# Fewer warm-up matmuls, x transposed by halves, and the first projections by column chunks, in a kernel of gated attention and feed-forward

## The chip, the cores and the metric

One core of a Trainium2 chip. The core has a matrix engine (TensorE, PE in the views; its weight loads are PEld), a vector engine (VectorE, DVE), a scalar engine (ScalarE, ACT), a general engine (GpSimd, POOL) and SyncE (SP), which issues most of the transfers. Each engine works through its own queue in order. The metric is device time of one launch in microseconds, lower is better.

## The reference

The input x has 2048 tokens of width 512. The output mixes two branches by a gate per token.

```python
x = A_x
g = _sigmoid((x * gate_w).sum(-1, keepdims=True))
a = _A_ref(x, A_wq, A_wk, A_wv, A_wo, A_beta)
b = _B_ref(x, B_W_gate, B_W_up, B_W_down)
return g * a + (1 - g) * b
```

Branch a is attention with 32 heads of width 16 in four segments of 512 tokens. In a segment each query attends causally to the keys of its own segment (softmax) and reads a memory of the earlier segments, a linear attention with phi(t) = t + 1 for t > 0 and exp(t) otherwise; a head's sigmoid(beta) mixes the two. At the end of a segment its keys and values are added to the memory. Branch b is a feed-forward net of width 1792: relu(x W_gate) times (x W_up), times W_down.

## The kernel before

**Tiles and stages.** The four segments (L = 512 tokens) are worked through with overlap. For a segment there are projections q, k and v (`proj_q`, `proj_k`, `proj_v`; four columns each, four matmuls of 128 x 512 to a column), attention by groups of eight heads (`attention`: score matmuls, an exponential on ScalarE, a causal mask on GpSimd, the product with v, then `normalise` on VectorE), `recall` and `memory` for the segments before, fourteen columns of the feed-forward net (`ffn_tasks`), and four output tiles (`out_tile`), which sum both branches in one PSUM bank. Matmuls of projections, feed-forward net and output all go through the helper `matmuls` (line 468), which cuts a sum into tasks of two matmuls (GM = 2); line 468 in a view is therefore any of them, and the operands tell which.

**The order.** Nothing is scheduled by the compiler. Every piece of work is a task in a list (`plan.add`) with an engine, an estimated duration, a key, the tasks it depends on and the PSUM banks or buffers it needs. `Plan.run` plays the list through with these estimates and picks, on each engine, the ready task with the lowest key; the instructions are then emitted in that order. Arrivals of transfers are tasks too, with estimated landing times in `LANDS`. A table `SHIFT` adds a number to the keys of single tasks, named by their place in the list. One unit of the key is 16,000 for the projections and the feed-forward net and 14,800 for attention.

**The start.** The transfers are issued first: x of segment 0 in two halves of tokens (`load_halves`, line 303, one half on SyncE's queue and one on ScalarE's), wq in two halves of its rows in the same way, then wk on SyncE's and wv on ScalarE's queue, then the feed-forward weights, gate_w, and x of the later segments, which a transposing transfer brings in as xT. For segment 0 xT is made on the chip instead (`x0_tasks`, line 479): TensorE first runs ten matmuls on a tile of zeros (`heat`, line 777; they write PSUM banks that nobody reads), then sixteen 128 x 128 transposes, four to each of the four column chunks of x, into one PSUM bank per chunk. Each chunk is copied to xT when its four transposes are done, chunks 0 and 2 by VectorE, 1 and 3 by ScalarE (line 492). In the plan the transposes wait for both halves of x, and every projection of segment 0 waits for all four copies and, for q, for both halves of wq. The gate's sums over x (line 420, four per segment, on VectorE) read the untransposed x.

Of the kernel before, what the change touches and what calls it, by code (L numbers as in the profile page):

```python
# [7 lines left out]
BF16 = mybir.dt.bfloat16  # L8
# [21 lines left out]
RH = 16  # L30

SHIFT = {
    21: -90000, 25: -170000, 29: -240000, 31: 210000, 52: 30000, 55: -10000, 58: -140000,
    74: 40000, 81: 90000, 85: 33000, 87: 80000, 88: -40000, 94: -80000, 115: 80000, 121: 100000,
    145: 130000, 204: -20000, 207: -50000, 210: -20000, 213: -3000, 222: -20000, 227: 270000,
    231: 1500, 234: 15600, 237: 30000, 240: -120000, 243: 11999, 246: 2000, 249: -10000,
    252: -14000, 255: 12999, 261: 28000, 264: -2000, 267: 30000, 270: 15000, 273: 28000,
    276: -10000, 279: 20000, 282: -2000, 300: -120000, 312: 24999, 324: -80000, 339: 80000,
    351: -50000, 354: 60000, 364: -20000, 372: -20000, 377: -50000, 379: 70000, 380: -40000,
    383: -100000, 385: 20000, 398: 10000, 400: 100000, 401: 10000, 404: 16000, 406: -130000,  # L40
    407: -4000, 480: -200000, 481: -190000, 544: 50000, 553: -18000, 556: 6000, 559: -30000,
    562: 2000, 565: -10000, 574: 19000, 583: -20000, 586: -10000, 589: -30000, 592: 9000,
    595: 10000, 598: 27000, 604: 2000, 607: -10000, 610: -4000, 613: -3000, 619: -10000,
    628: 21000, 631: -10000, 637: 29999, 661: 69999, 673: 70000, 686: 180000, 687: 150000,
    688: 100000, 689: -100000, 701: -120000, 704: 140000, 705: 110000, 709: -280000, 714: 15000,
    722: -6000, 727: -60000, 735: 15000, 737: 150000, 748: 8000, 751: -90000, 754: -60000,
    757: -10000, 796: -180000, 800: 90000, 801: 10000, 830: -160000, 831: -20000, 834: 140000,
    869: 30000, 903: 5000, 906: 40000, 909: -3000, 915: -15000, 921: -20000, 924: -10000,
    927: 10000, 930: 30000, 933: 10000, 936: 30000, 942: 30000, 945: -30000, 951: -10000,
    957: -20000, 963: -30000, 969: -20000, 972: 30000, 978: 40000, 984: 24000, 987: 209999,  # L50
    999: 110000, 1011: 60000, 1037: -230000, 1038: 60000, 1039: -260000, 1042: -100000,
    1046: -60000, 1047: 50000, 1052: -40000, 1054: -90000, 1057: 30000, 1062: -80000,
    1067: 56000, 1072: -60000, 1077: -50000, 1082: -70000, 1090: 50000, 1093: -20000,
    1096: 20000, 1134: -30000, 1170: 40000, 1239: 14000, 1242: 90000, 1247: 119999, 1248: 99999,
    1251: 10000, 1254: 60000, 1257: -20000, 1263: -2000, 1266: 20000, 1272: 50000, 1275: 60000,
    1278: 140000, 1284: 50000, 1290: 20000, 1293: -70000, 1296: -30000, 1299: -30000,
    1323: 159999,
}


# [154 lines left out]
def kernel(  # L215
# [69 lines left out]
    def work():  # L285
        return plan.one("ps", range(7, -1, -1))


    LANDS = dict(n0=4500, q=5950, k=9300, v=9750, g0=11800, u0=13300, gw=13900, g1=15200, u1=16700,
                 x1=18400, g2=20400, u2=21600, g3=22800, u3=24000, d0=27700, d1=30400, o=31800, n1=33400,  # L290
                 x2=35200)

    def arrival(name):
        return plan.add("in_" + name, 0.0, 0.0, None, lat=LANDS[name])

# [7 lines left out]
    def load_halves(dst, src, k, name):  # L303
        src = src.rearrange("(c p) n -> p c n", p=P)
        nc.sync.dma_start(out=dst[:, 0:k // 2], in_=src[:, 0:k // 2])
        nc.scalar.dma_start(out=dst[:, k // 2:k], in_=src[:, k // 2:k])
        return arrival(name)

    def load_xT(seg):
        nc.sync.dma_start_transpose(out=xT[seg % 3][:], in_=x[seg * L:(seg + 1) * L, :])  # L310
# [13 lines left out]
        return load(nc.sync, wd_sb[:, a:b, :],  # L324
                    B_W_down.rearrange("(c p) n -> p c n", p=P)[:, a:b, :], name)

    got_n[0] = load_halves(xn[0], x[0:L, :], 4, "n0")
    got_q = load_halves(wq_sb, A_wq, NC, "q")
    got_k = load_cols(nc.sync, wk_sb, A_wk, 0, D, "k")
    got_v = load_cols(nc.scalar, wv_sb, A_wv, 0, D, "v")  # L330
# [3 lines left out]
    got_gw = arrival("gw")  # L334
    load_gu(1)
    load_xT(1)
    got_x[1] = [arrival("x1")]
    junk = sb([P, L], BF16, "junk")
    nc.vector.memset(junk[:], 0.0)
    load_gu(2)  # L340
# [1 line left out]
    got_d = [load_wd(0, 7, "d0"), load_wd(7, NF, "d1")]  # L342
    got_o = load_cols(nc.sync, wo_sb, A_wo, 0, D, "o")
    load_xn(1)
    got_n[1] = arrival("n1")
    load_xT(2)
    got_x[2] = [arrival("x2")]
    plan.add("SP", 33100, -1e9, None)


# [64 lines left out]
    def gate_tasks(seg):  # L415
# [3 lines left out]
        for t in range(4):  # L419
            zs.append(plan.add("DVE", 690, key, lambda t=t: nc.vector.scalar_tensor_tensor(  # L420
                junk[:], xn[seg % 2][:, t, :], 1.0, gwb[:], ALU.mult, ALU.mult,
                accum_out=zc[:, 4 * seg + t:4 * seg + t + 1]), [got_n[seg], got_gw], 60, lock=True))
        att["xn", seg] = zs
        b = plan.add("DVE", 90, key, lambda: nc.vector.tensor_scalar(
            zc[:, cols], zc[:, cols], 80.0, -80.0, ALU.min, ALU.max), zs, DVL, lock=True)
# [33 lines left out]
            lock=seg > 0)  # L459


    def matmuls(key, deps, sl, ops, start=True, stop=True, prev=None, width=L, need=()):
        n = len(ops)
        for k in range(0, n, GM):
            def emit(k=k):
                for q in range(k, min(k + GM, n)):
                    lhsT, rhs = ops[q]()
                    nc.tensor.matmul(bank(sl)[:, 0:width], lhsT=lhsT, rhs=rhs,  # L468
                                     start=(start and q == 0), stop=(stop and q == n - 1))
            first = prev is None  # L470
            m = min(k + GM, n) - k
            t = plan.add("PE", 215.8 * width / L * m, key - (0 if first else CONT), emit, deps,
                         PEL, need=[sl] + list(need) if first else ())
            if not first:
                t.deps.append((prev, 0.0))
            prev, deps = t, ()
        return prev

    def x0_tasks():
        done = []  # L480
        for c in range(NC):
            sl = work()

            def pe(c=c, sl=sl):
                tp = bank(sl).bitcast(BF16)
                for t in range(4):
                    nc.tensor.transpose(tp[:, t * P:(t + 1) * P], xn[0][:, t, c * P:(c + 1) * P],
                                        ident[:])
            a = plan.add("PE", 240, K(-9), pe, [got_n[0]], PEL, need=[sl])
            cp = nc.scalar.copy if c % 2 else nc.vector.tensor_copy  # L490
            done.append(plan.add(
                "ACT" if c % 2 else "DVE", 430, K(-9), lambda c=c, sl=sl, cp=cp: cp(  # L492
                    xT[0][:, c, :], bank(sl).bitcast(BF16)[:, 0:L]),
                [a], DVL, frees=[sl]))
        return done

    def proj_mm(w, c, seg):
        return [lambda ci=ci: (w[:, ci, c * P:(c + 1) * P], xT[seg % 3][:, ci, :])
# [11 lines left out]
    def proj_q(seg, c):  # L510
        u, sl = 4 * seg + c, work()
        i = u % RQ
        key = K(4 * seg + c - 2 - (2 if seg else 0))
        war = [att.get(("pv", u - RQ)), att.get(("recall", u - RQ))]
        a = matmuls(key, got_x[seg] + [got_q] + war, sl, proj_mm(wq_sb, c, seg))
        xread.append(a)
        prj["q", seg, c] = plan.add("DVE", 600, key - RQK, lambda: nc.vector.tensor_copy(  # L517
            QT[i][:], bank(sl)), [a], DVL, frees=[sl])
        if seg:
            es, b = phi_exp(key, sl, a)  # L520
            prj["pq", seg, c] = plan.add("DVE", 665, key + 500, lambda: phi(
                pqT[i][:], QT[i][:], ex1[es.i][:]), [b, prj["q", seg, c]], DVL, frees=[es],
                lock=True)

    def proj_k(seg, c):
        i, u, sl = seg % 2, 4 * seg + c, work()
        key = K(4 * seg + c - 2 - (2 if seg else 0), 10)
        war = [att.get(("pv", u - RQ)), att.get(("recall", u - RQ))]
        a = matmuls(key, got_x[seg] + [got_k] + war, sl, proj_mm(wk_sb, c, seg))
        xread.append(a)  # L530
        ks = plan.one("ktr")
        d = plan.add("DVE", 600, key - RQK, lambda: nc.vector.tensor_copy(ktr[ks.i][:], bank(sl)),  # L532
# [242 lines left out]
    warm = [plan.one("ps") for _ in range(8)]  # L775

    def heat():
        for k in range(10):
            nc.tensor.matmul(bank(warm[k % 8]), lhsT=junk[:, 0:P], rhs=junk[:], start=True,  # L779
                             stop=True)  # L780
    plan.add("PE", 5280, -1e9, heat, lat=0, need=warm, frees=warm)
    got_x[0] = x0_tasks()
    for seg in range(NSEG):
        if seg > 1:
            got_n[seg] = plan.add("SP", 520, KA(4 * seg - 4), lambda seg=seg: load_xn(seg),
                                  att.get(("xn", seg - 2), []), 3500)
        if seg == 3:
            got_x[seg] = [plan.add("SP", 1900, K(4 * seg - 6), lambda seg=seg: load_xT(seg),
                                   list(xr0), 2200)]
        gate_tasks(seg)  # L790
        for c in range(NC):
            proj_q(seg, c)
            proj_k(seg, c)
        for t in range(4):
            proj_v(seg, t)
        for c in range(NC):
            if seg:
                recall(seg, c)
            attention(seg, c)
            if seg < NSEG - 1 and c == MEM:  # L800
                memory(seg, 4 * seg + c)
        ffn_tasks(seg)
        if seg == 0:
            xr0 = list(xread)
# [37 lines left out]
```

The softmax here doesn't subtract the row's maximum and nothing guards it: scores larger than these inputs give would overflow.

## Time and profile before

| | |
|---|---|
| median of 13 runs | 278.47 us (278.33 to 280.68) |
| the profiled execution's own time | 278.12 us |
| its span, first to last instruction | 276.3 us |
| busy: TensorE / VectorE / ScalarE / GpSimd | 265.4 / 207.7 / 195.9 / 87.3 us |
| first warm-up matmul starts | 1.25 us |
| first transpose of x starts | 5.49 us |
| first projection matmul starts | 7.46 us |
| first score matmul starts | 13.44 us |

Times in the profile count from the span's start. A row of the view in time gives start, duration, engine, line of the kernel, operation, what is written and read, and how many; in brackets stands how long the engine had been idle and what ended that. Matmuls overlap in their records, so their durations add up to more than the time they take; their pace is read from the distance of their starts. The chain of waits follows the work that ended last back to the start. The view by stretches gives busy time of each engine between two moments.

### The profile page before, as it was taken

The numbers are of one execution on the slowest core, as the hardware profiler recorded it, in microseconds if no ns is written. First come the engines' busy times: TensorE is split into PE (matmuls) and PEld (weight loads), VectorE is DVE, ScalarE is ACT, GpSimd is POOL, SyncE is SP. The second block draws the span as 40 slices with busy tenths as digits, with TensorE's granted clock in tenths as the row PEclk, the third lists the DMA queues.
The fourth block names the chain that finished last, engine by engine and source line by source line (L and its number), as shares of the span: only waits on it lengthen the run. The fifth ranks groups of instructions, "written<-read, shape, count | busy, mean of one in ns | idle before, by whom it ended". The sixth has DMA issues, their size and how long they took to land.

```text
span 276.3 us, 5510 instructions
## 1 busy us (share of the span) xinstructions
PE 265.4 (96%) x2178; PEld 113.3 (41%) x2214; DVE 207.7 (75%) x456; ACT 195.9 (71%) x176; POOL 87.3 (32%) x139
## 2 busy tenths in 40 slices
PE   8899999989999999999999999999999999999995
PEld 4343444433343433434343434343444334344543
DVE  3688989999898869698998768999228785638322
ACT  2299898968897778899996878778847776734100
POOL 5013333432424342534333343333301435230000
PEclk9999999999999999999999999999999999999999
DMA  7999955100411100100001000000000000000001
GB/s 234 328 281 346 258 81 168 11 15 0 96 23 20 23 19 21 21 0 19 4 0 34 8 19 5 19 19 2 0 0 4 19 21 19 21 0 0 2 28 48
DMA packets 27993, 15.46 MB, mean 56 GB/s; under 512 B 15680, under 2 KB 27968, under 8 KB 27968
## 3 DMA queue, kind: packets, MB, share of 16 engines
q1 hardware_dynamic: 26752, 14.06, 19.3%
q10 hardware_dynamic: 1216, 1.06, 1.2%
q8 instruction: 17, 0.28, 0.4%
q14 instruction: 8, 0.07, 0.1%
HBM read 9.86 MB, written 2.10 MB: 43 GB/s over the span
## 4 chain that ended last, share of the span: by engine, by line
PE 81%; DVE 10%; ACT 4%; issue 4%; DVEq 0%; ACTq 0%
PE ps L468 63%; PE ps L578 8%; PE ps L620 6%; PE ps L681 2%; ACT E L598 2%; PE ps L779 2%; DVE hT L743 1%; ACT ex L507 1%; DVE ktr L532 1%; DVE T L651 1%; DVE junk L420 1%; DVE QT L517 1%; ACT rgr L737 1%; DVE och L656 1%; ACT Vp L561 0%
## 5 line engine op out<-in xcount | busy, mean ns | idle before, releaser
L598 ACT ACTIVATE E<-ps 128x2048 bf16<-128x2048 f32 x80 | 150.6, 1882 | 31.5 <-PE ps L578 26.6
L607 POOL TENSOR_SCALAR_AFFINE_SELECT E<-E 128x512 bf16<-128x512 bf16 x128 | 83.6, 668 | 157.8 <-ACT E L598 157.8
L743 DVE TENSOR_TENSOR hT<-ps,rgr 128x512 bf16<-128x512 f32 x56 | 38.2, 685 | 29.3 <-PE ps L468 21.4
L468 PE MATMUL ps<-xT,wg_sb 128*128 128x512 bf16 x214 | 56.9, 380 | 1.3 <-issue 0.3
L468 PE MATMUL ps<-xT,wu_sb 128*128 128x512 bf16 x220 | 55.8, 380 | 0.8 <-issue 0.5
L468 PE MATMUL ps<-wd_sb,hT 128*128 128x512 bf16 (+1 forms) x233 | 54.5, 367 | 0.8 <-issue 0.5
L737 ACT ACTIVATE rgr<-ps 128x512 bf16<-128x512 f32 x56 | 32.6, 604 | 16.2 <-PE ps L468 11.5
L651 DVE STREAM_TRANSPOSE T<-ps 128x512 f32<-128x512 f32 x56 | 37.3, 694 | 7.1 <-PE ps L620 5.0
L468 PEld LDWEIGHTS <-hT 128*128 128x128 bf16 x238 | 21.9, 98 | 25.1 <-issue 3.9
L468 PEld LDWEIGHTS <-wg_sb 128*128 128x128 bf16 x224 | 20.6, 98 | 26.5 <-issue 4.7
L468 PEld LDWEIGHTS <-wu_sb 128*128 128x128 bf16 x224 | 20.5, 98 | 26.4 <-issue 4.6
L765 DVE TENSOR_SCALAR osr<-ps,ngcol 128x512 bf16<-128x512 f32 (+1 forms) x17 | 12.1, 709 | 13.9 <-PE ps L468 13.9
L620 PE MATMUL ps<-E,Vp 128*17 128x256 bf16 (+3 forms) x512 | 20.8, 300 | 0.4 <-DVE hT L743 0.4
L507 ACT ACTIVATE ex<-ps 128x512 bf16<-128x512 f32 x24 | 14.4, 600 | 9.6 <-DVE ktr L532 7.2
L656 DVE TENSOR_TENSOR och<-T,cfr 128x512 bf16<-128x512 f32 x28 | 20.6, 736 | 0.4
L578 PE MATMUL ps<-QT,KTe 32*128 32x512 bf16 (+3 forms) x256 | 17.3, 302 | 0.7 <-ACT E L598 0.4
L578 PE MATMUL ps<-QT,KTo 32*128 32x512 bf16 (+3 forms) x256 | 17.1, 300 | 0.5 <-ACT E L598 0.4
L468 PE MATMUL ps<-wv_sb,xT 128*128 128x512 bf16 x62 | 16.7, 380 | 0.6 <-DVE T L651 0.4
L468 PE MATMUL ps<-wo_sb,oT 128*128 128x512 bf16 (+1 forms) x65 | 17.0, 367 | 0.3 <-issue 0.2
L468 PE MATMUL ps<-xT,wk_sb 128*128 128x512 bf16 x57 | 16.6, 381 | 0.4 <-ACT ex L507 0.3
L468 PE MATMUL ps<-xT,wq_sb 128*128 128x512 bf16 x59 | 16.0, 379 | 0.8 <-DVE xT L492 0.4
L620 PEld LDWEIGHTS <-Vp 128*17 128x17 bf16 x512 | 10.9, 91 | 12.9 <-issue 3.9
(70 smaller groups left out, 189.4 us busy)
## 6 DMA issues: line engine op xcount, KB each, us to landing
out_dram<-osr SPq DMA_DIRECT2D x15, 128.0 KB, 1.7
wd_sb<-in_B_W_down_dram SPq DMA_DIRECT2D x2, 896.0 KB, 10.0
xn<-in_A_x_dram SPq DMA_DIRECT2D x3, 512.0 KB, 3.6
wg_sb<-in_B_W_gate_dram SPq DMA_DIRECT2D x2, 512.0 KB, 8.7
wu_sb<-in_B_W_up_dram SPq DMA_DIRECT2D x2, 512.0 KB, 9.0
wg_sb<-in_B_W_gate_dram SPq DMA_DIRECT2D x2, 384.0 KB, 4.7
wu_sb<-in_B_W_up_dram SPq DMA_DIRECT2D x2, 384.0 KB, 5.8
wk_sb<-in_A_wk_dram SPq DMA_DIRECT2D x1, 512.0 KB, 7.3
```

The costliest lines, as they stand in the source:

```text
L468: nc.tensor.matmul(bank(sl)[:, 0:width], lhsT=lhsT, rhs=rhs, start=(start and q == 0), stop=(stop and q == n - 1))
L507: return es, plan.add("ACT", 478, key + 500, lambda: nc.scalar.activation(ex1[es.i][:], bank(sl), ACT.Exp), [a], ACL, need=[es], frees=[sl])
L578: nc.tensor.matmul(ps[:, j * L + off:j * L + off + n], lhsT=kt[32 * j:32 * j + 32, kb * P:(kb + 1) * P], rhs=QT[i][32 * j:32 * j + 32, kb ...
L598: nc.scalar.activation(Ef[:, e0 * L:e1 * L], ps[:, e0 * L:e1 * L], ACT.Exp, scale=SCALE),
L607: nc.gpsimd.affine_select(out=m, in_=m, compare_op=ALU.is_ge, fill=0.0, base=0, pattern=[[0, 4], [1, P]], channel_multiplier=-1)
L620: nc.tensor.matmul(bank(sl)[32 * j:32 * j + HW, kb * P:kb * P + w], lhsT=Vp[i][:, kb, 8 * c + 2 * j + r, 0:HW], rhs=E[(NFILL * u + f) % RE ...
L651: done.append(plan.add("DVE", 633, key - RL, lambda r=r, sl=sl: nc.vector.transpose(T[ts.i][:, r], bank(sl)), [a] + done, 60 if r else 0, ...
L656: nc.vector.tensor_tensor(och[ds.i].rearrange("p (q r e) -> p r q e", r=2, e=DH), t()[:, :, :, 0:DH], cfr[cs.i][:, :, :, None].to_broadcas ...
L681: a = plan.add("PE", 216, key + r, lambda r=r, sl=sl: nc.tensor.matmul(bank(sl), lhsT=mbd[i][:, c, r].rearrange("p j e -> p (j e)"), rhs=p ...
L737: r = plan.add("ACT", 478, key - RL, lambda sl=gsl, rs=rs: nc.scalar.activation(rgr[rs.i][:], bank(sl), ACT.Relu), [g], ACL, frees=[gsl])
L743: nc.vector.tensor_tensor(hT[hs1.i][:], bank(sl), rgr[rs.i][:], ALU.mult)),
L765: b = plan.add("DVE", 95 + 1.12 * w, key - RL, lambda: nc.vector.tensor_scalar(osr[os.i][:, 0:w], bank(sl)[:, 0:w], ngcol[:, tt:tt + 1], N ...
```

## The change

It does five things.

1. `heat` runs seven matmuls instead of ten.
2. The two halves of x and of wq become arrivals of their own (`na`, `nb`, `qa`, `qb`), so that tasks can wait for one of them. The transfers themselves are the same.
3. `x0_tasks` issues the sixteen transposes in another order: first those of chunks 0 and 1 for the first half of the tokens, which wait for the first half of x alone, then those of chunks 0 and 1 for the second half, then chunk 2, then chunk 3. Chunks 0, 2 and 3 are copied by VectorE, chunk 1 by ScalarE.
4. `matmuls` takes a table `chunk` of what each single matmul needs. A q projection's first pair of matmuls now waits for chunks 0 and 1 and the first half of wq, its second pair for chunks 2 and 3 and the second half; k projections wait in the same way for the chunks of x. The v projections and the feed-forward net wait for all four chunks as before.
5. The table `SHIFT` is replaced by another one (166 entries before, 141 after). Since three tasks more stand at the front of the list, a place n of the table before corresponds to n + 3.

The diff, the table cut to its first lines:

```diff
 SHIFT = {
-    21: -90000, 25: -170000, 29: -240000, 31: 210000, 52: 30000, 55: -10000, 58: -140000,
-    74: 40000, 81: 90000, 85: 33000, 87: 80000, 88: -40000, 94: -80000, 115: 80000, 121: 100000,
...
+    22: -80000, 23: 130000, 38: 50000, 62: -90000, 69: -10000, 75: 10000, 80: 7000, 83: -50000,
+    88: -110000, 123: 30000, 151: 30000, 170: -30000, 179: 40000, 203: 70000, 207: -10000,
...
 }
-    LANDS = dict(n0=4500, q=5950, k=9300, v=9750, g0=11800, u0=13300, gw=13900, g1=15200, u1=16700,
+    LANDS = dict(na=4300, nb=4600, qa=5650, qb=6050, k=9300, v=9750, g0=11800, u0=13300, gw=13900, g1=15200, u1=16700,
...
         nc.sync.dma_start(out=dst[:, 0:k // 2], in_=src[:, 0:k // 2])
         nc.scalar.dma_start(out=dst[:, k // 2:k], in_=src[:, k // 2:k])
-        return arrival(name)
+        return [arrival(name + h) for h in "ab"]
...
-    def matmuls(key, deps, sl, ops, start=True, stop=True, prev=None, width=L, need=()):
+    def matmuls(key, deps, sl, ops, start=True, stop=True, prev=None, width=L, need=(), chunk={}):
...
-            t = plan.add("PE", 215.8 * width / L * m, key - (0 if first else CONT), emit, deps,
+            t = plan.add("PE", 215.8 * width / L * m, key - (0 if first else CONT), emit,
+                         list(deps) + [d for q in range(k, k + m) for d in chunk.get(q, ())],
                          PEL, need=[sl] + list(need) if first else ())
...
     def x0_tasks():
-        done = []
+        sl = [work() for _ in range(NC)]
+
+        def flip(pairs):
+            for c, t in pairs:
+                nc.tensor.transpose(bank(sl[c]).bitcast(BF16)[:, t * P:(t + 1) * P],
+                                    xn[0][:, t, c * P:(c + 1) * P], ident[:])
+        pairs = [(c, t) for h in range(2) for c in range(2) for t in (2 * h, 2 * h + 1)]
+        pairs += [(c, t) for c in (2, 3) for t in range(4)]
+        ends = {0: 6, 1: 8, 2: 12, 3: 16}
+        done, at = [], 0
+        plan.add("PE", 430, K(-9), lambda: flip(pairs[0:4]), got_n[0][:1], need=sl[0:2])
+        at = 4
         for c in range(NC):
...
+            a = plan.add("PE", 107.0 * (ends[c] - at), K(-9) + c + 1,
+                         lambda a=at, b=ends[c]: flip(pairs[a:b]), got_n[0], PEL,
+                         need=sl[c:c + 1] if c > 1 else ())
+            a.deps.append((plan.tasks[-2], 0.0))
+            at = ends[c]
+            done.append(a)
+        return [plan.add(
+            "ACT" if c == 1 else "DVE", 485 if c == 1 else 345, K(-9),
+            lambda c=c, cp=nc.scalar.copy if c == 1 else nc.vector.tensor_copy: cp(
+                xT[0][:, c, :], bank(sl[c]).bitcast(BF16)[:, 0:L]),
+            [done[c]], DVL, frees=[sl[c]]) for c in range(NC)]
...
-        a = matmuls(key, got_x[seg] + [got_q] + war, sl, proj_mm(wq_sb, c, seg))
+        a = matmuls(key, war, sl, proj_mm(wq_sb, c, seg),
+                    chunk={ci: [got_x[seg][ci], got_q[ci // 2]] for ci in range(NC)})
...
-        a = matmuls(key, got_x[seg] + [got_k] + war, sl, proj_mm(wk_sb, c, seg))
+        a = matmuls(key, [got_k] + war, sl, proj_mm(wk_sb, c, seg),
+                    chunk={ci: [got_x[seg][ci]] for ci in range(NC)})
...
-        for k in range(10):
+        for k in range(7):
             nc.tensor.matmul(bank(warm[k % 8]), lhsT=junk[:, 0:P], rhs=junk[:], start=True,
                              stop=True)
-    plan.add("PE", 5280, -1e9, heat, lat=0, need=warm, frees=warm)
+    plan.add("PE", 4250, -1e9, heat, lat=0, need=warm, frees=warm)
```

## The prediction

> **What bounds the kernel now.** I read the page's shares first, then the chain of waits from the start, the engines in time over the first 13 us, the DMA issues, and last the busy time by stretch.
>
> ```profile
> PE 265.4 (96%) x2178; PEld 113.3 (41%) x2214; DVE 207.7 (75%) x456; ACT 195.9 (71%) x176; POOL 87.3 (32%) x139
> PE 81%; DVE 10%; ACT 4%; issue 4%; DVEq 0%; ACTq 0%
> ```
>
> TensorE is busy for 265.4 of 276.3 us and holds 81% of the chain. What takes time off TensorE counts, unless the 10% of VectorE stands in its place.
>
> ```profile
> 1.25 4.45 PE ps L779 x10
> 5.70 1.17 PE ps L487 x12
> 6.87 0.02 issue
> 6.89 0.44 DVE xT L492
> 7.32 0.14 issue
> 7.46 4.06 PE ps L468 x18
> ```
>
> Start, duration, work. Until 7.46 us the chain is warm-up matmuls, transposes of x, one copy, and then the projections. No DMA is in it. The rows in time (start, duration, engine, line) say why:
>
> ```profile
> 5.49 1.58 PE L487 MATMUL ps<-ident,xn 128*128 128x128 bf16 x16
> 6.16 1.07 ACT L492 COPY xT<-ps 128x512 bf16<-128x512 bf16 x2 [1.93 <-PE ps L487]
> 6.89 0.75 DVE L492 COPY xT<-ps 128x512 bf16<-128x512 bf16 x2 [3.14 <-PE ps L487]
> 7.46 2.32 PE L468 MATMUL ps<-xT,wq_sb 128*128 128x512 bf16 x10 [0.39 <-DVE xT L492]
> 9.62 0.59 PE L468 MATMUL ps<-xT,wk_sb 128*128 128x512 bf16 x2
> 11.54 0.69 DVE L532 CAST ktr<-ps 128x512 bf16<-128x512 f32 x1 [1.40 <-PE ps L468]
> ...
> wk_sb<-in_A_wk_dram SPq DMA_DIRECT2D x1, 512.0 KB, 7.3
> wv_sb<-in_A_wv_dram ACTq DMA_DIRECT2D x1, 512.0 KB, 7.9
> xn<-in_A_x_dram ACTq DMA_DIRECT2D x1, 256.0 KB, 3.6
> xn<-in_A_x_dram SPq DMA_DIRECT2D x1, 256.0 KB, 3.3
> wq_sb<-in_A_wq_dram ACTq DMA_DIRECT2D x1, 256.0 KB, 4.7
> wq_sb<-in_A_wq_dram SPq DMA_DIRECT2D x1, 256.0 KB, 4.2
> ```
>
> Issue plus time to landing gives: x first half 0.80 + 3.3 = 4.1, second half 0.80 + 3.6 = 4.4; wq halves 1.32 + 4.2 = 5.5 and 1.31 + 4.7 = 6.0; wk 1.81 + 7.3 = 9.1; wv 1.85 + 7.9 = 9.75. So x lies there from 4.4 and TensorE takes it up at 5.49, because ten warm-up matmuls stand ahead of it; the projections could have their weights at 6.0 and start at 7.46.
>
> ```profile
> core 0: us, PE busy (x) PEld busy (x) DVE busy (x) ACT busy (x) POOL busy (x), PEclk, DMA share, GB/s
> 40.00:80.00 40.00, 37.60 (x365) 15.93 (x369) 37.39 (x87) 33.62 (x33) 13.60 (x21) 1.00 0.23 55
> 120.00:160.00 40.00, 39.47 (x326) 16.06 (x331) 35.83 (x76) 33.76 (x28) 15.31 (x24) 1.00 0.05 11
> ```
>
> Between 40 and 80 us TensorE idles 2.40 us while VectorE is busy for 37.39 of 40; between 120 and 160 it idles 0.53. So the order of the work still has some room in the first of these stretches.
>
> **The pace of TensorE at the start.** The granted clock column says 1.00 from the first slice, but the pace does not: the warm-ups start every 0.424 us (first 1.25, tenth 5.07), where projections go 0.216 apart (10 from 7.46 to 9.62). Transposes start 0.107 apart up to 6.6 us and 0.055 after. I go by the pace: half speed until 6.6, that is 5.35 us after the first matmul.
>
> **The change, part by part.**
> Seven warm-ups instead of ten: three at 0.424 = 1.27 us less. They end at 1.25 + 7 x 0.424 = 4.22, just behind the first half of x (4.1).
> Transposes by halves: still sixteen. The first four need the first half only, so the second (4.4) is there before the fifth begins at 4.65; half-wise waiting saves at most 4.4 - 4.22 = 0.2 us. At 0.107 each they end at 4.22 + 1.71 = 5.93. No DMA is added or moved.
> The copies: a transpose takes 0.314, and a copy starts some 0.03 behind it (before: fourth transpose at 5.81, copy at 6.16). Column 0 ends with the sixth, 4.755 + 0.314, so its copy runs 5.10 to 5.52 (0.42, VectorE row); column 1 with the eighth, ScalarE 5.31 to 5.90 (0.59); columns 2 and 3 on VectorE 5.74 to 6.16 and 6.17 to 6.59. One copy moves from ScalarE to VectorE: +0.42 on an engine that idles 3.14 us just there; uncovered it would cost 0.42. ScalarE has its table (2.95 to 4.23) behind it by then.
> The first projections: chunk 0 waits for the last of TensorE's own transposes (5.93), its copy plus 0.15 (5.67) and wq (5.5): 5.93. Chunk 1 needs 5.90 + 0.15 = 6.05 and at half speed is due at 6.36. Chunk 2 needs 6.31 and the second half of wq (6.0), due about 6.67; chunk 3 needs 6.74, due 6.89. If one is late, the other half-columns of q stand behind it in the in-order queue, but the hand-made order puts a pair of chunks as its own task, so another column's first pair can go ahead. From 5.93 to 6.6 TensorE does at half speed 0.67 us, worth 0.33 at full, so it is as if the projections started at 6.27: a gain of 7.46 - 6.27 = **1.2 us**.
> What is late next: sixteen q matmuls from 6.27 last 16 x 0.216 = 3.45, to 9.7; wk (9.1) is then there, and wv (9.75) is needed a k column later. VectorE idles 1.40 before the first k copy at 11.54, which now comes sooner. The gain is not caught by a transfer.
>
> The order table is replaced whole: 166 entries before, 141 after; counted by the task they move, 75 tasks are in both and 5 with the same value. So from 14 us on nearly everything may stand elsewhere, with the same instructions. The page cannot show the new order. Bounds: if segment 1 (about 40 to 80) gets as smooth as 120 to 160, 2.40 - 0.53 = 1.87 us are gained; if a later segment gets as rough as 40 to 80, 1.87 are lost. I take 0, since both tables are of one kind, and keep both ends for the range.
>
> Sum: 278.12 (the profiled execution's own time, span 276.3) - 1.2 = 276.9; the median of the runs is 0.35 above that execution, so 278.47 - 1.2 = **277.3**.
>
> **Where a rule speaks against it.** The transposes before ran at the slow pace for 1.1 us behind the last warm-up, and the grant at 6.6 fell among them. The Trainium skill (TensorE: Matmul & The Clock Gate, Part 4: PE-mode transpose) says that transposes don't count as busy work for the gate, and Part 1 of the same page asks for about 3.4 us of sustained work: seven warm-ups last 2.97, so by that rule the count would be unfinished when the transposes begin, and the projections would start it again or finish it. By the page's figure, counted from 5.93, full speed would come at 9.3, the half-speed stretch would cost (9.3 - 6.6)/2 = 1.35, and the sum would be 278.6 (an estimate from that page). If transposes count as matmuls do, the sum above stands. No row before separates the two.
>
> **Rivals.**
> 1. The full speed comes later. The grant is tied to plain matmul work, not to time. For it: only warm-ups ran before the grant, ten of them, and three go. Least: the missing 1.27 us are made up by projections from 5.93 to 7.2, and the same 1.1 us pass as before: 8.3. Half speed from 6.6 to 8.3 costs half of it, 0.85: net -0.35, 278.1. Most: the count of 5.35 us starts anew at 5.93, to 11.28: (11.28 - 6.6)/2 = 2.34, net +1.1, 279.6. Between them 1.6, net +0.4: **278.9**. It eats the gain from a grant at 9.0 on. Against it: TensorE has no gap over 0.2 us either way, and 12 of 13 runs lie within 0.41 us, so the grant moves little from run to run.
> 2. The new order makes a second segment as rough as 40 to 80: +1.87 - 1.2 = +0.67, **279.1**, slower. It happens among VectorE's work: the four gate sums of segment 1 (L420, 0.68 us each) move forward by 10,000 to 100,000 units, into 24 to 60 us, where VectorE is already 33.86 of 36 busy (same view); what feeds TensorE stands behind them. It decides from 1.2 + 0.56 = 1.8 us of new TensorE idle time on. Against it: TensorE's idle time over 8 to 272 us is 264.00 - 257.77 = 6.23 in all, so it would have to grow by 30%.
> 3. The gain is swallowed where VectorE bounds: what TensorE has in hand at 40 us is waited for between 52 and 80, and VectorE isn't earlier: **278.4**. Against it: VectorE's own first k copy moves up too.
> 4. The new order also smooths segment 1 by half of 1.87: 277.3 - 0.9 = **276.4**.
> That the change doesn't do what it says: if the half-wise wait were on both halves, it would cost 0.2 us only.
>
> **How the numbers follow.** Forecast 0.44, with its own range of 276.7 to 277.9 (half of the 1.2, or half again). Rival 1: 0.14. Rival 2: 0.14. Rival 3: 0.13. Rival 4: 0.15. A measurement tells about 0.2%, 0.56 us, from no change: faster is under 277.9, slower over 279.0. Faster: 0.42 of the forecast, all of rival 4, 0.03 of rivals 1 and 3: 0.60. Slower: half of rival 1 (0.07), most of rival 2 and the rougher orders around it: 0.24. Same: the rest, 0.16. The range takes 276.2 (just beyond rival 4) to 279.1 (rival 2's middle) and leaves out the rest of rivals 1, 2 and 4, about 0.2.
>
> **What would show it.** In the profile after: seven warm-ups 0.424 apart to 4.2, the first transpose at 4.2 to 4.5, the first q matmul between 5.9 and 6.2; starts 0.216 apart from about 6.6 on. If they are still 0.42 apart at 8, rival 1 is at work. The first k copy near 10.3 instead of 11.54; if it stays near 11.5, rival 3. TensorE's idle time over 40 to 80 and 120 to 160 against 2.40 and 0.53 shows rivals 2 and 4. The prediction is wrong if the projections start early and the last matmul still does not end 1 us sooner than the 273.2 of before.

## The result and the profile after

The changed kernel takes 277.56 us in the median of 15 runs (277.19 to 278.26), the kernel before 278.38 in 67 runs taken along with it. The ratio is 0.9969, with a 95% interval of 0.9961 to 0.9977: 0.3% faster, 0.82 us where 1.2 were forecast. The profiled execution after is the longest of the 15, 278.26 us with a span of 276.4; a median execution has a span of 275.7.

First the page of the changed kernel, shares of the span and of the chain; then the chain in time (start, duration, work):

```profile
PE 264.7 (96%) x2175; PEld 112.9 (41%) x2211; DVE 208.5 (75%) x457; ACT 195.5 (71%) x175; POOL 86.8 (31%) x139
PE 80%; DVE 9%; ACT 4%; DMA 3%; issue 3%; ACTq 0%; DVEq 0%
...
1.86 9.15 DMA wv_sb<-in_A_wv_dram
11.05 1.05 PE ps L463 x4
12.13 0.70 DVE ktr L538
12.86 0.61 ACT ex L511
13.50 1.02 PE ps L463 x4
```

Before, no transfer was in the chain. Now it begins with one: the load of wv, issued at 1.86 us and landed at 11.0. Everything that the change does at the start lies beside that transfer. The rows of the engines in time show what waits for it:

```profile
1.25 3.17 PE L785 MATMUL ps<-junk 128*128 128x512 bf16 x7 [1.25 <-DVE mcol_e L352]
4.32 1.89 PE L480 MATMUL ps<-ident,xn 128*128 128x128 bf16 x16
6.00 3.71 PE L463 MATMUL ps<-xT,wq_sb 128*128 128x512 bf16 x16
9.55 0.59 PE L463 MATMUL ps<-xT,wk_sb 128*128 128x512 bf16 x2
11.05 0.61 PE L463 MATMUL ps<-wv_sb,xT 128*128 128x512 bf16 x2 [0.91 <-DMA wv_sb<-in_A_wv_dram]
11.50 0.59 PE L463 MATMUL ps<-xT,wk_sb 128*128 128x512 bf16 x2
11.93 1.46 PE L463 MATMUL ps<-wv_sb,xT 128*128 128x512 bf16 x5
13.50 0.59 PE L463 MATMUL ps<-xT,wg_sb 128*128 128x512 bf16 x2
...
5.18 0.42 DVE L497 COPY xT<-ps 128x512 bf16<-128x512 bf16 x1 [1.44 <-PE ps L480]
5.82 0.85 DVE L497 COPY xT<-ps 128x512 bf16<-128x512 bf16 x2 [0.21 <-PE ps L480]
12.13 0.69 DVE L538 CAST ktr<-ps 128x512 bf16<-128x512 f32 x1 [1.69 <-PE ps L463]
```

The first projection starts at 6.00 instead of 7.46, and all sixteen q matmuls and the first two of k are done by 9.98; before, twelve matmuls were done at 10.05. Then TensorE comes to v, and wv is not there. The same place before:

```profile
10.05 1.03 PE L468 MATMUL ps<-wv_sb,xT 128*128 128x512 bf16 x4
12.91 0.59 PE L468 MATMUL ps<-xT,wk_sb 128*128 128x512 bf16 x2 [0.33 <-ACT ex L507]
```

After, behind the first v pair stands the second k pair, which needs nothing but wk; the k copy on VectorE (12.13) waits for it, an exponential on ScalarE for the copy (12.86), and at 13.50 a feed-forward matmul for the bank that this exponential frees. So the first k copy comes at 12.13, later than the 11.54 of before. A median execution is 0.7 us shorter; if all of that lies ahead of v, as in the runs below, its first k copy comes at 11.4, hardly sooner than before.

### The profile page after: what moved, and what is told of

It is laid out like the page before. It is cut to its first block, busy times and chain, and to the rows that moved or that the text cites. A ratio compares the mean times of both kernels' runs of the same rounds, so it can differ in the third digit from the quotient of the medians.

```text
span 276.4 us, 5505 instructions
## 1 busy us (share of the span) xinstructions
PE 264.7 (96%) x2175; PEld 112.9 (41%) x2211; DVE 208.5 (75%) x457; ACT 195.5 (71%) x175; POOL 86.8 (31%) x139
## 3 DMA queue, kind: packets, MB, share of 16 engines
q10 hardware_dynamic: 1216, 1.06, 1.1%
## 4 chain that ended last, share of the span: by engine, by line
PE 80%; DVE 9%; ACT 4%; DMA 3%; issue 3%; ACTq 0%; DVEq 0%
PE ps L463 63%; PE ps L584 8%; PE ps L626 7%; DMA wv_sb<-in_A_wv_dram 3%; PE ps L687 2%; ACT ex L511 2%; ACT E L604 1%; DVE hT L749 1%; DVE ktr L538 1%; ACT rgr L743 1%; DVE QT L522 1%; DVE och L662 1%; DVE pkT L506 1%; DVE pkT L507 1%; PE ps L705 1%
## 5 line engine op out<-in xcount | busy, mean ns | idle before, releaser
L463 PE MATMUL ps<-wd_sb,hT 128*128 128x512 bf16 (+1 forms) x229 | 52.8, 366 | 1.6 <-issue 1.1
L463 PE MATMUL ps<-wo_sb,oT 128*128 128x512 bf16 (+1 forms) x66 | 16.2, 366 | 0.2 <-issue 0.2
## 6 DMA issues: line engine op xcount, KB each, us to landing
wd_sb<-in_B_W_down_dram SPq DMA_DIRECT2D x2, 896.0 KB, 10.2
```

The costliest lines, as they stand in the source:

```text
L463: nc.tensor.matmul(bank(sl)[:, 0:width], lhsT=lhsT, rhs=rhs, start=(start and q == 0), stop=(stop and q == n - 1))
```

## The experiments

Two measures are used throughout. "v" is the start of the first v matmul, "rest" the span minus v; both are read from each kernel's profile. Times are medians, ratios are against the kernel before on the same chip. On the chips used the kernel before has medians between 278.27 and 278.51 us, so two kernels are compared by their ratios where 0.2 us matters; a difference of 0.001 in the ratio is 0.28 us. Theory 1 is that v, held by the landing of wv, and a rest that no longer moves make up the time; theory 2, the rival, that the start's gain arrives whole and something is lost later.

| kernel | time | ratio (95%) | v | rest |
|---|---|---|---|---|
| before | 278.38 | 1 | 10.05 | 266.30 |
| after | 277.56 | 0.9969 (0.9961 to 0.9977) | 11.05 | 265.35 |
| a_ten_warm | 277.98 | 0.998 (0.997 to 0.9989) | 10.23 | 265.37 |
| b_seven_warm | 278.36 | 1.0003 (0.999 to 1.0016) | 10.51 | 266.30 |
| a_wv_early | 277.75 | 0.9977 (0.9969 to 0.9986) | 10.12 | 265.61 |
| a_plain_start | 277.71 | 0.9983 (0.9968 to 0.9997) | 10.66 | 265.36 |
| a_ffn_later | 277.66 | 0.9976 (0.9967 to 0.9984) | 10.22 | 265.59 |
| a_no_warm | 278.75 | 1.0014 (1.0005 to 1.0022) | 11.88 | 265.37 |
| a_transpose_warm | 277.70 | 0.997 (0.9958 to 0.9982) | 10.56 | 265.36 |
| b_new_order | 278.94 | 1.0021 (1.0011 to 1.0031) | 10.41 | 266.89 |
| a_old_order | 297.48 | 1.0691 (1.0668 to 1.0714) | 10.37 | 284.91 |
| b_seven_k_first | 278.17 | 0.9984 (0.9975 to 0.9993) | 10.64 | 265.61 |
| a_k_first | 277.00 | 0.9944 (0.993 to 0.9959) | 10.58 | 264.66 |
| a_k_first_ffn_later | 278.01 | 0.9988 (0.9979 to 0.9997) | 9.82 | 266.34 |

**a_ten_warm: the three warm-ups put back, the order kept.**

```diff
-        for k in range(7):
+        for k in range(10):
```

> The changed kernel with ten warm-up matmuls again, all else in the same order. Theory 1 (the gain of the start is cut off at about 10 us, because the first v matmuls wait for wv, which landed at 11.0 us in the changed kernel's profile, and wk's second pair stands behind them): TensorE comes to v 1.27 us later, at 11.25, and no longer waits; of the 1.27 us only 0.2 to 0.8 show: 277.8 to 278.4. Theory 2 (the start's gain arrives whole, and the new order loses some elsewhere): 277.56 + 1.27 = 278.8.

277.98, inside theory 1's range and 0.8 below theory 2's: of the 1.27 us that three warm-ups take, 0.42 show by the medians and 0.31 by the ratios (the interval overlaps that of the changed kernel, and excludes 1.27). Its profile is of a shorter execution than the changed kernel's:

```profile
4.98 1.06 PE L480 MATMUL ps<-ident,xn 128*128 128x128 bf16 x16
6.00 3.67 PE L463 MATMUL ps<-xT,wq_sb 128*128 128x512 bf16 x16
9.50 0.59 PE L463 MATMUL ps<-xT,wk_sb 128*128 128x512 bf16 x2
10.23 0.61 PE L463 MATMUL ps<-wv_sb,xT 128*128 128x512 bf16 x2
```

Sixteen transposes take 1.06 us here and 1.89 in the changed kernel: full speed came at 4.5 us in this execution, so that ten warm-ups and q at 6.00 go together, and v, forecast at 11.25, starts at 10.23. The span is 275.6 against 276.4, and the whole difference stands in v: 11.05 - 10.23 = 0.82. The rests agree within 0.02 us.

**b_seven_warm: seven warm-ups in the kernel before, its order kept.**

```diff
-        for k in range(10):
+        for k in range(7):
```

> The kernel before with seven warm-up matmuls, all else in the same order. Theory 1: its thirteenth matmul is already a v matmul; with q from about 6.3 it gets there at 8.9 and waits for wv until 9.8 at least, so hardly 0.3 us remain of the 1.1: 278.0 to 278.3. Theory 2: 277.2 to 277.4. If the three warm-ups were needed for the clock, matmuls at 0.42 us pace beyond 6.6 us and no gain.

278.36, no gain at all: just above the range of theory 1 and 1 us above that of theory 2.

```profile
6.40 2.32 PE L468 MATMUL ps<-xT,wq_sb 128*128 128x512 bf16 x10 [0.18 <-DVE xT L492]
9.35 0.60 PE L468 MATMUL ps<-xT,wk_sb 128*128 128x512 bf16 x2 [0.63 <-DMA wk_sb<-in_A_wk_dram]
10.51 1.02 PE L468 MATMUL ps<-wv_sb,xT 128*128 128x512 bf16 x4 [0.55 <-DMA wv_sb<-in_A_wv_dram]
```

q starts 1.06 us earlier than before; two waits for weights of 0.63 and 0.55 us take it all back in this execution, a longer one (279.05). The old order has only ten q matmuls ahead of k, the new one sixteen.

**a_old_order and b_new_order: each start with the other's table, every entry put on the same task.**

In a_old_order the old place n of the table becomes n + 3 (n + 2 for the two tasks ahead of the transposes), in b_new_order the reverse:

```diff
 SHIFT = {
-    22: -80000, 23: 130000, 38: 50000, 62: -90000, 69: -10000, 75: 10000, 80: 7000, 83: -50000,
...
+    23: -90000, 34: 210000, 55: 30000, 58: -10000, 61: -140000,
...
```

```diff
 SHIFT = {
-    21: -90000, 25: -170000, 29: -240000, 31: 210000, 52: 30000, 55: -10000, 58: -140000,
...
+    20: -80000, 21: 130000, 35: 50000, 59: -90000, 66: -10000,
...
```

> The new start with the table of order shifts of before, each entry put on the same task (the two entries for the transposes left out). If the gain is the start's alone: 277.3 to 277.8. If the new table is needed, because the old one fits other moments: over 278.4, up to 281.

> The kernel before with the new table, each entry on the same task. If a table fits only the start that it was made for, as a_old_order (297.5) says: well over 280. If the new table is simply the better one: under 278.

a_old_order takes 297.48 us. It starts like the changed kernel, with sixteen q matmuls and two of k ahead of v, and loses in the rest:

```profile
5.88 3.62 PE L607 MATMUL ps<-xT,wq_sb 128*128 128x512 bf16 x16
9.33 0.59 PE L607 MATMUL ps<-xT,wk_sb 128*128 128x512 bf16 x2
10.37 1.04 PE L607 MATMUL ps<-wv_sb,xT 128*128 128x512 bf16 x4 [0.44 <-DMA wv_sb<-in_A_wv_dram]
...
80.00:100.00 20.00, 13.32 (x113) 5.29 (x115) 9.44 (x21) 15.31 (x12) 8.07 (x13) 0.72 0.08 9
```

Its waits of TensorE, in the view of who waited for whom (us in total, times, longest):

```profile
PE ps L728 <- ACT E L748: 11.8, 7, 2.7
PE ps L607 <- DMA xT<-in_A_x_dram: 2.7, 1, 2.7
```

Seven times the score matmuls wait for the exponential before them, with nothing put between to fill the time. Between 80 and 100 us TensorE is busy for 13.32 of 20 us and its granted clock is 0.72; it stands at one half from 77.5 to 91.1 us. How much of the 19 us is due to the lower clock was not separated from the waits. b_new_order misses the other way: not far over 280, only 278.94, 0.2% slower than before. The new table on the old start costs 0.6 us, the old table on the new start 19. Neither part of the change is a gain without the other.

```profile
8.79 1.03 PE L584 MATMUL ps<-xT,wq_sb 128*128 128x512 bf16 x4
9.66 0.59 PE L584 MATMUL ps<-xT,wk_sb 128*128 128x512 bf16 x2
10.41 0.60 PE L584 MATMUL ps<-wv_sb,xT 128*128 128x512 bf16 x2 [0.16 <-DMA wv_sb<-in_A_wv_dram]
```

In b_new_order fourteen matmuls stand ahead of v (twelve of q from 6.88 on, of which the last four are shown, and two of k), against twelve before and eighteen after. So it is the new start, under either table, that brings six more of them ahead of v.

**a_plain_start: both halves of x and all four copies waited for, order and seven warm-ups kept.**

```diff
-        pairs = [(c, t) for h in range(2) for c in range(2) for t in (2 * h, 2 * h + 1)]
+        pairs = [(c, t) for h in range(2) for c in range(2) for t in (2 - 2 * h, 3 - 2 * h)]
...
-        a = matmuls(key, war, sl, proj_mm(wq_sb, c, seg),
+        a = matmuls(key, war, sl, proj_mm(wq_sb, c, seg)[::1 if seg else -1],
...
     order = plan.run()
+    k = next(i for i, t in enumerate(order) if t.eng == "PE" and t.n > got_x[0][-1].n)
+    cps = [t for t in order if any(t is c for c in got_x[0])]
+    order = [t for t in order[:k] if t not in cps] + cps + [t for t in order[k:] if t not in cps]
```

The last lines emit the four copies ahead of the first projection.

> The changed kernel, same order of work and seven warm-ups, but the first transposes use the second half of x (so both halves are waited for) and each q sum of segment 0 begins with chunk 3, which is copied last (so all four copies are waited for). By now theory 1 reads: the time is the moment of the first v matmul, which is when wv has landed (10.3 us in the median), plus a rigid rest of 265.4 us. q then starts near 6.8 instead of 6.0 and v is reached at 10.6 to 10.7: 0.2 to 0.4 us more than 277.56, 277.8 to 278.0. If waiting by halves and by chunks carries its full worth: 278.3 or more.

q starts at 6.78, as expected 0.8 later, and v at 10.66. The time is 277.71, a little under the forecast of theory 1 and under the 278.3 of the full 0.8. Against the changed kernel it is 0.15 us by the medians and 0.39 by the ratios, and the intervals overlap: what waiting by halves and chunks is worth is not told from nothing.

**a_wv_early and a_ffn_later: wv sooner, in two ways.**

```diff
-    got_v = load_cols(nc.scalar, wv_sb, A_wv, 0, D, "v")
+    wv_src = A_wv.rearrange("(c p) n -> p c n", p=P)
+    nc.sync.dma_start(out=wv_sb[:, 0:2], in_=wv_src[:, 0:2])
+    nc.scalar.dma_start(out=wv_sb[:, 2:4], in_=wv_src[:, 2:4])
+    got_v = arrival("v")
```

```diff
+    hold = dram.tile([1, D], BF16, name="hold")
+    nc.sync.dma_start(out=hold[:], in_=wq_sb[0:1, 0, :])
     load_gu(0)
```

> The changed kernel with wv loaded in two halves, one on each queue, ahead of the feed-forward weights; same order of work. Theory 1: wv lands before 9.7 us, the wait of 0.91 us in front of v goes, 276.6 to 277.2. Theory 2: 277.5, no change, since the gain is lost elsewhere.

> The changed kernel with one transfer of 1 KB out of wq put on SyncE's queue ahead of the feed-forward weights, so that these are issued only when the first half of wq is there (5.5 us), and wk and wv have the DMA engines to themselves until then; same order of work. Theory 1: wv lands at 9 or before, v starts at 10.0 without a wait, 0.3 to 0.4 us less than 277.56: 277.1 to 277.3, unless the feed-forward weights come too late for their first matmul at 13. Theory 2 (v's wait does not matter): 277.56 or more.

Both missed theory 1's range, and their times are those that theory 2 allows. In a_wv_early the second half of wv landed at 10.0 and v still waited 0.27 us: two halves on two queues were no faster in its profile than the one transfer in some others (9.9 to 11.0). In a_ffn_later wv was there at 9.3 and nothing was waited for at the start, but its profile shows full speed only at about 6.7 and v at 10.22. In both the rest is 0.24 us longer: some 67 us after v VectorE falls 0.30 us behind, which it does not do in the kernels with a rest of 265.35 to 265.37; why was not found. That is a loss further on, as theory 2 has it, so the rest is not rigid when the loads are issued otherwise, and these two do not tell the theories apart.

**a_k_first and b_seven_k_first: the wait filled instead of shortened.** TensorE's queue gets the second k pair ahead of the first v pair. The lines are those of b_seven_k_first, which also runs seven warm-ups; a_k_first moves the same two matmuls.

```diff
     order = plan.run()
+    k0 = xread[1]
+    v0 = next(t for t in order if t.n in [v.n - 1 for v in xread[8:12]])
+    order.remove(k0)
+    order.insert(order.index(v0), k0)
```

> The changed kernel with the second pair of the first k column moved ahead of the first v pair on TensorE, nothing else. These two matmuls (0.43 us) need only wk and then run while wv is still on its way. Theory 1 (v's start, set by wv, plus a rigid rest): the rest gets 0.43 us shorter and v starts no earlier than 10.41; with 10.34 in the median before, 0.3 to 0.4 us less than 277.56: 277.1 to 277.3. Theory 2 (the wait for wv costs nothing that counts): 277.5 to 277.6.

> The kernel before with seven warm-ups and with the second pair of the first k column moved ahead of the first v pair. Seven warm-ups alone gave nothing here (278.36), since v waits for wv from 9.8 on. Theory 1: the two k matmuls fill 0.43 us of that wait: 277.9 to 278.1. Theory 2: 278.3 to 278.4.

a_k_first takes 277.00 us, 0.56% less than before (0.9944, 0.993 to 0.9959), better than both kernels. It gains more than theory 1 forecast, and theory 2 has no place for it.

```profile
5.50 3.63 PE L463 MATMUL ps<-xT,wq_sb 128*128 128x512 bf16 x16 [0.25 <-DVE xT L497]
9.55 1.04 PE L463 MATMUL ps<-xT,wk_sb 128*128 128x512 bf16 x4 [0.43 <-DMA wk_sb<-in_A_wk_dram]
10.58 1.90 PE L463 MATMUL ps<-wv_sb,xT 128*128 128x512 bf16 x8
12.31 0.59 PE L463 MATMUL ps<-xT,wg_sb 128*128 128x512 bf16 x2
```

The rest is 264.66, shorter by 0.70: 0.43 for the two matmuls that now stand ahead of v, and about 0.28 because the feed-forward matmul at 12.31 follows v at once, where the changed kernel waited for the exponential behind the late k copy. By the ratios a_k_first gains 0.70 us over the changed kernel, as much as its rest is shorter. In b_seven_k_first the same edit gives 278.17, between the two forecasts: 0.19 us under b_seven_warm by the medians and 0.5 by the ratios, with a rest shorter by 0.69. The intervals of the two just touch, so this run alone decides nothing. v began at 10.64 there, after a wait for wv of 0.44.

**a_k_first_ffn_later: the edits of a_k_first and of a_ffn_later together.**

> Both edits together: the first k column whole ahead of v, and the feed-forward weights issued only when the first half of wq is there. In a_k_first TensorE waited 0.43 us for wk (9.5), in a_ffn_later wk and wv were there at 8.8 and 9.3 and no load was waited for. If the loads are what is left to gain at the start: v at 9.9 to 10.4 instead of 10.58, and 0.2 us come back in the later stretch that a_ffn_later showed (rest 265.59 instead of 265.36): 276.7 to 277.0. If the clock decides what is left: as a_k_first, 277.0 to 277.3.

A miss: 278.01. v starts at 9.82 with no wait, the earliest of all, and the next load is late:

```profile
8.96 1.03 PE L465 MATMUL ps<-xT,wk_sb 128*128 128x512 bf16 x4
9.82 1.89 PE L465 MATMUL ps<-wv_sb,xT 128*128 128x512 bf16 x8
12.22 0.60 PE L465 MATMUL ps<-xT,wg_sb 128*128 128x512 bf16 x2 [0.51 <-DMA wg_sb<-in_B_W_gate_dram]
```

The feed-forward weights that were held back are waited for in their turn, and so is gate_w behind them: VectorE idles 1.30 us until it can start the gate's sums at 14.13, and the next k copy stands behind three of these. The rest is 266.34, longer by 1.68 than in a_k_first, and 0.3 of that comes again at 66 us after v, as in the two kernels above.

**a_no_warm and a_transpose_warm: what the clock counts.**

```diff
-        for k in range(7):
+        for k in range(0):
```

```diff
-        for k in range(7):
-            nc.tensor.matmul(bank(warm[k % 8]), lhsT=junk[:, 0:P], rhs=junk[:], start=True,
-                             stop=True)
+        for k in range(28):
+            nc.tensor.transpose(bank(warm[k // 4]).bitcast(BF16)[:, (k % 4) * P:(k % 4 + 1) * P],
+                                junk[:, (k % 4) * P:(k % 4 + 1) * P], ident[:])
```

> The changed kernel without any warm-up matmul, same order. If transposes count for the clock as matmuls do, half speed ends 2 to 5 us after the first transpose at 4.3, between 6.3 and 9.3: v is reached between 10.0 and 11.5, time 277.6 to 278.7. If they don't count, the grant comes only after the projections have run for that long, from 6 us on, to 9 or 11: 278.7 to 279.5.

> The changed kernel with 28 transposes of the tile of zeros in place of the seven warm-up matmuls; at 0.107 us each they take the same 3 us. If transposes count for the clock as matmuls do: half speed ends between 4.5 and 6.7 us as in the runs so far, 277.4 to 278.0. If they don't count: as without warm-ups, half speed until 9 to 10 us, 278.5 to 279.

Without warm-ups q runs at half speed until about 10.2 us (sixteen matmuls from 5.86 to 11.45) and the time is 278.75; both lie where they were expected if transposes don't count, the time just so. With transposes as warm-ups the time is 277.70, what matmuls as warm-ups give within the intervals.

```profile
1.42 3.15 PE L785 MATMUL ps<-ident,junk 128*128 128x128 bf16 x28 [1.42 <-POOL ident L348]
4.36 1.91 PE L480 MATMUL ps<-ident,xn 128*128 128x128 bf16 x16
6.07 4.23 PE L463 MATMUL ps<-xT,wq_sb 128*128 128x512 bf16 x16
10.13 0.59 PE L463 MATMUL ps<-xT,wk_sb 128*128 128x512 bf16 x2
```

Sixteen q matmuls take 4.06 us from start to start of the next work, 3.45 at full speed; the 0.61 us more are three matmuls at half speed, so full speed came at 7.3, only 1.2 us after the first plain matmul. With plain warm-ups it never came sooner than 2.8 us after the first of them. In both kernels full speed came 5.9 to 6.0 us after the first transpose (1.42 to 7.3, 4.18 to 10.2), later than the 2.8 to 5.4 us after the first of plain matmuls. Since 1.2 us of plain matmuls were enough only behind 44 transposes, transposes count for the clock at least in part; that they count as much as matmuls is not shown. The moments are from one profile each; the medians, 277.70 against 278.75, bear out that the 28 transposes work as warm-ups.

## Why the prediction was right, point by point

**The start** came out as worked out. Warm-ups to 4.2, first transpose at 4.32 (forecast 4.22), copies at 5.18 and 5.82 (5.10 and 5.74), first q matmul at 6.00 (5.93).

**The step that was mis-sized** is "What is late next", with its end "The gain is not caught by a transfer". It let wv be needed "a k column later" than 9.7 and took wv's landing from one execution, 9.75. In the new order v stands behind half a k column, so it is reached at 9.98, and wv landed at 11.0 in the execution profiled after, at 9.9 to 10.6 in the variants with the same loads (issue at 1.86 plus 8.0 to 8.7). With a rest of 265.36 a median span of 275.7 puts v at 10.3; for the kernel before some 276.5 and 266.30 put it at 10.2. So v starts no earlier than before. The gain is instead that more work is done ahead of it: six matmuls, 6 x 0.216 = 1.30 us. Of this the rest gets 266.30 - 265.36 = 0.94, and 0.36 is lost again. Where was not located: the wait of 0.28 at 13.50 can hardly be it, since the kernel before waits 0.33 for an exponential too, at 12.91. 0.94 less 0.1 for v is 0.84, against 0.82 measured. That wv alone holds v back in every execution is not shown: in the profiles of a_plain_start, a_no_warm and a_transpose_warm nothing waits for it, and v comes when TensorE gets there.

**Its own sign of being wrong** came up in the profile: the projections start early, and the last matmul ends at 273.3, no sooner than the 273.2 of before. In a median execution, 0.7 us shorter, it ends 0.6 sooner, still not the 1 us asked for. That the time lies in the range and near the forecast is therefore in part luck: the whole start was to come 1.2 us sooner, v included, and only the work ahead of v did.

**The warm-ups** were costed at 1.27 us on the path. By themselves they are worth 0.0 in the old order (b_seven_warm) and 0.3 to 0.4 in the new (a_ten_warm): their worth depends on what the order can do before wv lands, and the trace of before showed that limit, with v at 10.05 and wv at 9.75.

**The order table**, taken as 0, is not neutral: without it the new start is a loss of 19 us, though the six matmuls stand ahead of v there too (a_old_order). The forecast had no branch for that, since both parts came together. Neither of its two bounds was reached; in the view by stretches (stretch, length, busy time of TensorE first):

```profile
40.00:80.00 40.00, 38.69 (x377) 16.28 (x382) 37.61 (x85) 36.11 (x37) 14.73 (x23) 1.00 0.24 54
120.00:160.00 40.00, 38.82 (x321) 15.99 (x323) 33.44 (x72) 32.98 (x28) 14.91 (x24) 1.00 0.06 15
```

TensorE idles 1.31 us instead of 2.40 in the first and 1.18 instead of 0.53 in the second stretch. Segment 1 got smoother by 1.09 us, about what rival 4 had (half of 1.87), and the later stretch rougher by 0.65, a third of what rival 2 had. Over 8 to 272 us in all, TensorE idles 264.00 - 256.65 = 7.35 us instead of 6.23, and 0.91 of the difference is the wait for wv. So the new order is not smoother than the old one.

**Rival 1**, a later clock, did not happen in the execution profiled: half speed ended at 6.2 us in the changed kernel and at 6.6 before. But the forecast's fixed 6.6 and its argument that the grant moves little from run to run did not hold: with plain warm-ups it came anywhere between 4.0 and 6.7 us. Nor has TensorE "no gap over 0.2 us": before, it idles 0.39 us in front of the first projection, behind the grant. The rule that was weighed, that transposes don't count as busy work (the Trainium skill, TensorE: Matmul & The Clock Gate, Part 4: PE-mode transpose), would fit a_no_warm by itself but not a_transpose_warm, and the measurement decides: a start with 28 transposes reaches full speed 1.2 us after its first plain matmul. **Rival 3** had the right outcome for part of the gain and, as far as the profiles show, the wrong cause: the gain is cut at the wait for wv at 10 us, not by VectorE at 40.

## What to carry to other kernels

When a start is made shorter, go along the queue to the first instruction whose data come by a transfer, and count how much work stands ahead of it: only that work can be gained, and its landing should be taken from several executions. Before making the transfer faster, put whatever is ready ahead of the wait in an in-order queue; here two matmuls moved gave 0.56 us more (0.70 by the ratios), while three attempts to hurry or delay loads gave nothing. A table fitted to one start can cost more with another than the start gains, here 19 us: change and measure both together.

## What the runs showed of the hardware

- The same load of wv, issued at 1.85 to 1.86 us behind the same transfers, landed at 9.75 in the profile of before, at 11.0 in that of after, and between these in nine more kernels.
- Behind the first v matmul the work repeats itself closely: over five kernels with one order and the same transfers, one profile each, the rest is 265.35 to 265.37 us, with v between 10.23 and 11.88. Two more with this order, whose loads are issued otherwise, have 265.59 and 265.61.
- With seven or ten warm-up matmuls, full speed came between 4.0 and 6.7 us, 2.8 to 5.4 us after the first of them, and ten brought it no sooner than seven (4.5 to 6.6 and 4.0 to 6.7). The Trainium skill (the same page, Part 1: The HAM clock gate) puts the change at about 4 us, give or take half a microsecond, and calls the count of slow matmuls variable from run to run; the spread here is wider than the half.
- The column of the granted clock says 1.00 in these first microseconds, while the pace of the matmuls is half. In the traces that have a record of the clock it begins only with the change to full speed (6.2 us after, 6.6 before, 10.2 without warm-ups), where the pace changes too.
- In a_old_order TensorE waited for exponentials from 74.7 us on, 2.0 to 2.7 us at a time. Its granted clock fell to one half at 77.5 us and was full again at 91.1.
